# Attention fill work: halves ordered by the scalar engine's sequencer, transfers paced by exponentials, three vector-exponential stacks

## The chip, the cores and the metric

The kernel runs on one core of a Trainium2 chip. The core has TensorE (PE: matmuls), VectorE (DVE), ScalarE (ACT: exponentials), GpSimd (POOL, which here mostly issues transfers) and SyncE (SP, which issues the other transfers). Each engine works through its own list of instructions in order; between engines an instruction waits on semaphores. The metric is the device time of one execution, in microseconds (us).

## The reference

Two independent blocks share one output. Block A is attention with 32 query heads of width 16 over one common key and value head, for 2048 positions; block B is a short causal convolution, a product, and a long causal convolution done by Fourier transforms, for 512 channels.

```python
q = (x @ wq).reshape(B, S, H, Dh).transpose(0, 2, 1, 3)      # H = 32, Dh = 16, S = 2048
k = x @ wk; v = x @ wv                                       # one head for all
p = softmax(einsum("bhqd,bkd->bhqk", q, k) * Dh ** -0.5)
a = einsum("bhqk,bkd->bhqd", p, v).transpose(0, 2, 1, 3).reshape(B, S, H * Dh) @ wo
k_shift = sum(k_pad[:, t:t + S, :] * shift_k[:, 3 - t] for t in range(4))
kv = k_shift * v_B
y = irfft(rfft(kv, 2 * S) * rfft(ssm_k, 2 * S))[:S] + kv * ssm_D
out = concatenate([a, q_B * y], axis=-1)
```

## The kernel before

**Attention.** The 32 heads and 2048 queries are cut into 32 *stacks*. A stack is four heads by 512 queries, against 16 key tiles of 128 keys, so it has 32 *tiles* of 128 keys by 1024 query columns. For each tile PE makes the scores (eight matmuls, line 928) into one of two PSUM buffers `s`, ACT turns them into exponentials `p` (line 940, one instruction per tile), and some tiles later PE multiplies `p` with the values (line 964, "pv") into an accumulator pair `f`. After a stack's last tile VectorE copies the accumulator out (lines 973 and 974), and the sums and the unnormalised outputs go to DRAM. The loop `attend` writes this program one tile at a time; one pass of it is a *step*, and each step has one exponential. The two `s` buffers mean that the scores of tile t+1 wait until the exponential of tile t-1 is done.

**Fill work.** Everything else is written into the gaps of that loop by `_Fill`: the query projections, the transforms of block B (forward: `hT` and `a` against the table `ff`; backward: `sp` against `fi`), the output projection `wo`. Each of these is a Python generator, a "thread", that asks for PE matmul units or for VectorE time, or says `WAIT n`, which means 2n steps of nothing. `_Fill.turn` has a budget per step for PE and another for VectorE (850 ns per step). So the order on every engine is fixed when the program is written; nothing is rearranged at run time.

**Halves.** Most fill matmuls come through `halves` (line 243 is its matmul, line 255 its memset). A product is done as two halves: in the first, rows 0 to 63 of the PE array write one PSUM bank and rows 64 to 127 another; in the second half the two row groups change banks. The two row groups run side by side, so the second half may begin only when the last matmul of the first half is finished. The kernel orders this with a small VectorE memset of the tile `look`: the memset waits for the last matmul of the first half, and the first matmul of the second half waits for the memset. `yield WAIT, 0.5` puts the second half at least one step later.

**Vector exponentials.** In four stacks (`OWN_IN`, line 71) the last key tile's two exponentials are not made by ACT. The thread `own` (lines 1016 to 1027) has PE make those scores during the stack before, and VectorE evaluates a polynomial of degree five on them; `pv` then takes the result. Such a stack has 30 tiles for ACT instead of 32.

**Transfers.** POOL issues the loads of block B: the tables `ff` and `fi` (line 288), the long filter `hin` (line 316), rows of keys `kk` (lines 355 and 367), `tpb` (358), values `v` (380), gates `q` (442), and the stores `out` (463). SP issues the rest, among them the stack's queries `st` (884), the spill of two chunks of the transposed input to DRAM and its return (805, 811), and the small transfers of `heads`. A transfer is issued as soon as its queue reaches it and its buffer is free.

**Heads.** For each pair of stacks, `heads` loads the row sums `rl` and the outputs `of` from DRAM (1064, 1066), VectorE takes reciprocals (1070, 1071), these go to DRAM (`rd`, 1072) and come back spread over the partitions (`r`, 1077), and VectorE divides (1082). `WAIT` statements between these steps say how many steps later the consumer is written.

Of the kernel before, what the change touches and what calls it, by code (L numbers as in the profile page):

```python
# [8 lines left out]
F32 = mybir.dt.float32  # L9
# [4 lines left out]
AF = mybir.ActivationFunctionType  # L14
# [5 lines left out]
P = 128  # L20
# [3 lines left out]
DH = 16  # L24
NKT = S // P
NQ = 4 * H // 4
CB = 256
# [6 lines left out]
SC = XS * WS  # L34
# [28 lines left out]
LN2 = 0.6931471805599453  # L63
# [4 lines left out]

DOWN = 80
OWN = NKT - 1  # L70
OWN_IN = (27, 28, 29, 30)
OWN_AT, OWN_PV = 14, 8


# [31 lines left out]
WAIT = -1.0  # L106
# [3 lines left out]
class _Emit:  # L110
# [22 lines left out]
    def order(self, a, b):  # L133

        info = mybir.DependencyInfo(mybir.DependencyClass.Sync, mybir.DependencyReason.DATA)
        self.tc.add_manual_dep(a.ins, b.ins.name, info, reason="row halves change banks")

    def wide(self):
        return self.ps.tile([P, 2, 512], F32, tag="s", name=self.nm("x"))
# [87 lines left out]
    def halves(self, a, b, grain, dve=0):  # L227

        banks, look = [], None
        for half in range(2):  # L230
            n, k = 0, len(a)
            while n < k:
                g = yield (k - n) * grain, dve * half, CONT if banks else NEW, grain
                start = not banks
                if start:
                    f = self.pair()
                    banks += [f[:, 0, :], f[:, 1, :]]
                for m in range(n, n + g // grain):
                    for e in range(2):
                        out, (cols, w, x) = banks[half ^ e], (a, b)[half ^ e][m]  # L240
                        r = slice(64 * e, 64 * e + 64)
                        for j in range(0, P, 32):
                            y = self.nc.tensor.matmul(  # L243
                                out[j : j + 32, cols],
                                w[r, j : j + 32],
                                x[r],
                                start=half == m == 0,
                                stop=half == 1 and m == k - 1,
                            )
                            if look is not None:  # L250
                                self.order(y, look)
                                look = None
                n += g // grain
            if half == 0:
                look = self.nc.vector.memset(self.look, 0.0)  # L255
                self.order(look, y)
                yield WAIT, 0.5, CONT
        return banks
# [26 lines left out]
    def table(self, n, m2):  # L285
        t = self.w.tile([P, 2, 2, P], F32, tag="ft", bufs=FT, name=self.nm(n))
        for i in range(2):
            self.nc.gpsimd.dma_start(t[:, i], self.I[n][:, 2 * m2 + i])  # L288
        return t

    def s2(self, n, shape=(2, CB), dt=F32):
# [15 lines left out]
    def long_load(self, blk):  # L307

        nc = self.nc
        hin = self.w.tile([P, 8, 512], F32, tag="in", bufs=1, name=self.nm("hin"))  # L310
        for b in range(8):
            c0 = blk * CB + 32 * b
            for a in range(0, 4, 2):
                dst = hin[32 * a : 32 * a + 64, b, :]
                src = self.I["B_ssm_k"][c0 : c0 + 32, 512 * a : 512 * a + 1024].rearrange("r (a t) -> a r t", a=2)
                nc.gpsimd.dma_start(dst, src)
            yield WAIT, 1.5
        return hin

# [27 lines left out]
    def short_load(self, blk):  # L347
        nc, w = self.nc, self.w
        cs = slice(blk * CB, (blk + 1) * CB)
        tpb = w.tile([P, 4, CB], F32, tag="tp", bufs=1, name=self.nm("tpb"))  # L350
        kk = w.tile([P, 16, CB], F32, tag="in", bufs=1, name=self.nm("kk"))
        nc.gpsimd.memset(kk[0:1, 13:16, :], 0.0)
        for i in range(13, 16):
            for a, b in ((1, 16), (16, P)):
                nc.gpsimd.dma_start(kk[a:b, i, :], self.kr[a - 1 : b - 1, i, cs])
            yield WAIT, 0.5
        for i in range(4):
            nc.gpsimd.dma_start(tpb[:, i, :], self.skd[i : i + 1, cs].broadcast_to([P, CB]))
            yield WAIT, 0.5
        for m2 in range(2):  # L360
            self.rows(kk, blk, m2)
            yield WAIT, 0.5
        self.ld[blk] = tpb, kk

    def rows(self, kk, blk, m2):
        for i in (2 * m2, 2 * m2 + 1):
            self.nc.gpsimd.dma_start(kk[:, i, :], self.kr[:, i, blk * CB : (blk + 1) * CB])

    def short_products(self, blk, tpb, kk):

        nc, w = self.nc, self.w
        cs = slice(blk * CB, (blk + 1) * CB)
        for m2 in range(8):
# [19 lines left out]
            for i in (2, 1, 0):  # L393
                t = self.s2("t")
# [35 lines left out]
    def backward(self, blk, cx, places):  # L430

        nc, w = self.nc, self.w
        cs = slice(blk * CB, (blk + 1) * CB)
        g1, g2 = places
        ft, q = {i: self.table("fi", i) for i in range(2)}, {}

        def load(m2):
            if m2 > 1:
                ft[m2] = self.table("fi", m2)
            q[m2] = self.s2("q")  # L440
            for i in range(2):
                nc.gpsimd.dma_start(q[m2][:, i], self.qr[:, 2 * m2 + i, cs])

        load(0)
        load(1)
# [1 line left out]
        for m2 in range(8):  # L447
# [11 lines left out]
            b = yield from self.halves(*work, 2, 850)  # L459
# [265 lines left out]
    def prologue(self):  # L725
        nc = self.nc
# [6 lines left out]
        self.gm = self.c.tile([P, 18], F32, name="gm")  # L733
        nc.gpsimd.memset(self.gm, 0.0)
        self.qa, self.st, self.pt, self.qn, self.qs = {}, {}, {}, (0, 0), set()
        self.kst = self.c.tile([P, S], F16, name="kst")
        self.vx = self.c.tile([P, NKT, 32], F32, name="vx")
        self.look = self.c.tile([P, 4], F32, name="look")
# [61 lines left out]
    def spill(self):  # L800

        for c in range(2, 4):
            for i in range(8):
                yield WAIT, 0.5
                self.nc.sync.dma_start(self.xd[c - 2, :, i // 4, i % 4], self.xT[c][:, i // 4, i % 4])
        self.seen.add("spill")
        for c in range(2):
            yield from self.after(f"q{c}")
            for i in range(8):
                yield WAIT, 1  # L810
                self.nc.sync.dma_start(self.xT[c + 2][:, i // 4, i % 4], self.xd[c, :, i // 4, i % 4])
            self.seen.add(("x", c + 2))

    def hurry(self):
# [122 lines left out]
    def exp(self, u, s):  # L937

        self.pt[u] = self.w.tile([P, 2, 512], F32, tag="p", bufs=PB, name=self.nm("p"))
        self.nc.scalar.activation(self.pt[u], s, AF.Exp, scale=LN2 * DH**-0.5 / SC / SC)  # L940

    def pv(self, x, part, stop=False):

# [113 lines left out]
    def heads(self, G):  # L1057
# [18 lines left out]
        for i in range(0, 512, CB):  # L1076
            nc.sync.dma_start(r[:, i : i + CB], rows[:, i : i + CB].unsqueeze(1).broadcast_to([8, DH, CB]))
            yield WAIT, 1
        yield WAIT, 1.5
        for out, a, b, op in ((oc[:, 0], o, r, ALU.mult), (o, o, r, ALU.mult), (oc[:, 1], o, oc[:, 0], ALU.subtract)):  # L1080
            yield 0, 700
            nc.vector.tensor_tensor(out, a, b, op)
# [367 lines left out]
```

## Time and profile before

| what | value |
|---|---|
| time, median of 3 runs (lowest to highest) | 1049.73 us (1048.74 to 1056.47) |
| the profiled execution's own time | 1059.92 us |
| its span, first to last instruction | 1058.1 us |
| mean granted TensorE clock | 0.969 |
| PE / DVE / ACT / POOL busy | 960.1 / 760.1 / 955.2 / 171.3 us |
| exponentials (line 940) | 1016, 942.6 us busy, 66.1 us idle before them |

Busy time counts a stretch in which two instructions of an engine overlap once. The idle time of a group is what its engine stood still just before its instructions, with the releaser: the instruction whose semaphore ended most of it. An engine that is busy nine tenths of the time can still be waiting for another in the stretches that set the end, so the idle time in front of the exponentials, and what lies behind each piece of it, says more than the busy shares.

### The profile page before, as it was taken

How to read it: one execution, taken by the hardware profiler on the slowest of the kernel's cores; microseconds unless marked ns; L12 is line 12 of the kernel's file. 1: busy time of each engine (PE TensorE's matmuls, PEld its weight loads, DVE VectorE, ACT ScalarE, POOL GpSimd, SP SyncE). 2: the span in 40 equal slices, each digit the busy share in tenths (PEclk: the TensorE clock that was granted, in tenths of full speed). 3: DMA queues.
4: the chain of work that ended last, by engine and by line, in shares of the span. 5: the costliest groups of instructions: out<-in, count | busy, mean ns of one | idle time of the engine just before them, and what ended most of it. 6: DMA issues, size and time to landing. Idle time of an engine off the chain costs nothing.

```text
span 1058.1 us, 51250 instructions
## 1 busy us (share of the span) xinstructions
PE 960.1 (91%) x23455; PEld 469.8 (44%) x23455; DVE 760.1 (72%) x1094; ACT 955.2 (90%) x1032; POOL 171.3 (16%) x305
## 2 busy tenths in 40 slices
PE   8999998799998999899999989999889889888985
PEld 4345444344543444454444544444334344444452
DVE  4548854798536989888988657699898936775533
ACT  4799998699997999999998979999999998889883
POOL 2542214100031000012304243101000012201000
PEclk9899999899999999999999989999999999989998
DMA  6362435213142111212324243102211122210101
GB/s 227 117 188 75 140 90 116 67 52 96 48 108 64 61 45 51 65 57 71 116 72 140 83 129 101 51 29 64 84 40 32 60 71 66 87 59 28 46 4 43
DMA packets 69316, 83.11 MB, mean 79 GB/s; under 512 B 20800, under 2 KB 58278, under 8 KB 69094
## 3 DMA queue, kind: packets, MB, share of 16 engines
q1 hardware_dynamic: 47142, 43.51, 13.1%
q0 software_dynamic: 20320, 35.46, 11.9%
q8 instruction: 185, 3.03, 1.2%
q10 hardware_dynamic: 1632, 0.81, 0.3%
q14 instruction: 37, 0.30, 0.1%
HBM read 54.66 MB, written 25.03 MB: 75 GB/s over the span
## 4 chain that ended last, share of the span: by engine, by line
PE 36%; ACT 35%; issue 12%; DVE 11%; DMA 3%; POOL 2%; SPq 0%; ACTq 0%; POOLq 0%; DVEq 0%
ACT p L940 35%; PE f L964 16%; PE s L928 9%; PE f L243 8%; DVE sp L163 1%; DVE own L1027 1%; DVE ao L973 1%; DVE ao L974 1%; DVE sp L283 1%; DMA r<-rd 1%; DVE a L398 1%; POOL out L463 1%; DMA rd<-rl 1%; DMA xb<-in_A_x 1%; DVE t L389 1%
## 5 line engine op out<-in xcount | busy, mean ns | idle before, releaser
L940 ACT ACTIVATE p<-s 128x1024 f32<-128x1024 f32 x1016 | 942.6, 1064 | 66.1 <-PE s L928 62.9
L964 PE MATMUL f<-p,vx 64*32 64x512 f32 (+1 forms) x8880 | 561.3, 564 | 1.1 <-DVE sp L283 1.1
L928 PE MATMUL s<-st,kst 49*32 49x512 f16 x8128 | 432.1, 386 | 30.8 <-ACT p L940 26.1
L928 PEld LDWEIGHTS <-kst 49*32 49x32 f16 x8192 | 199.0, 91 | 392.3 <-issue 350.6
L964 PEld LDWEIGHTS f<-p,vx 64*32 64x32 f32 x8880 | 179.7, 108 | 37.6 <-issue 11.2
L163 DVE TENSOR_TENSOR sp<-sp 128x1024 f32<-128x1024 f32 x96 | 111.6, 1215 | 6.7 <-issue 6.1
L283 DVE COPY sp<-f 128x512 f32<-128x512 f32 x64 | 41.2, 685 | 42.4 <-PE f L243 42.0
L288 POOL DMA_DIRECT2D ff<-in_ff x64 | 34.3, 542 | 214.5 <-PE s L928 196.6
L463 POOL DMA_DIRECT2D out<-r x32 | 17.4, 550 | 287.0 <-DVE r L461 287.0
L243 PE MATMUL f<-wo,o 64*32 64x512 f16 x1440 | 56.6, 379 | 7.3 <-DVE look L255 6.0
L163 DVE TENSOR_TENSOR sp<-sp,sp 128x1024 f32<-128x1024 f32 x48 | 56.0, 1218 | 5.2 <-issue 3.9
L243 PE MATMUL f<-xT,wq 64*32 64x512 f16 x1344 | 51.8, 375 | 1.6 <-DVE look L255 1.2
L243 PE MATMUL f<-a,ff 64*32 64x256 f32 x1024 | 43.4, 386 | 9.2 <-DVE look L255 3.7
L243 PE MATMUL f<-hT,ff 64*32 64x256 f32 x1024 | 44.0, 381 | 8.5 <-issue 4.4
L243 PE MATMUL f<-sp,fi 64*32 64x256 f32 x1024 | 41.8, 387 | 9.8 <-DVE look L255 9.8
L973 DVE COPY ao<-f 128x512 f32<-128x512 f32 (+1 forms) x33 | 22.2, 673 | 29.5 <-PE f L964 29.4
L398 DVE TENSOR_TENSOR a<-a,t 128x512 f32<-128x512 f32 x48 | 33.1, 690 | 11.9 <-issue 10.2
L461 DVE TENSOR_TENSOR r<-f,q 128x256 f32<-128x256 f32 x32 | 12.1, 419 | 33.7 <-PE f L243 33.6
L389 DVE TENSOR_TENSOR t<-kk,tpb 128x512 f32<-128x512 f32 (+1 forms) x50 | 33.0, 662 | 3.0 <-issue 2.7
L380 POOL DMA_DIRECT2D v<-in_B_v x32 | 17.0, 537 | 100.3 <-DVE a L400 36.1
L243 PEld LDWEIGHTS <-o 64*32 64x32 f16 x1440 | 21.7, 93 | 23.2 <-DVE look L255 7.4
L243 PEld LDWEIGHTS f<-hT,ff 64*32 64x32 f32 x1024 | 20.9, 107 | 21.4 <-issue 9.1
(166 smaller groups left out, 751.0 us busy)
## 6 DMA issues: line engine op xcount, KB each, us to landing
ff<-in_ff POOLq DMA_DIRECT2D x64, 128.0 KB, 3.7
od<-ao SPq DMA_DIRECT2D x60, 128.0 KB
qd<-qp SPq DMA_DIRECT2D x48, 128.0 KB
st<-qd SPq DMA_DIRECT2D x62, 98.0 KB
kk<-in_B_k POOLq DMA_DIRECT2D x32, 128.0 KB, 3.8
v<-in_B_v POOLq DMA_DIRECT2D x32, 128.0 KB, 3.2
hin<-in_B_ssm_k POOLq DMA_DIRECT2D x32, 128.0 KB, 7.5
fi<-in_fi POOLq DMA_DIRECT2D x32, 128.0 KB, 3.0
```

What stands on the lines that cost most here:

```text
L163: v.tensor_tensor(part(out), part(a), part(b), op)
L243: y = self.nc.tensor.matmul(out[j : j + 32, cols], w[r, j : j + 32], x[r], start=half == m == 0, stop=half == 1 and m == k - 1,)
L283: self.nc.vector.tensor_copy(c[:, :, m + i, :], b[i].rearrange("p (q n) -> p q n", q=2))
L288: self.nc.gpsimd.dma_start(t[:, i], self.I[n][:, 2 * m2 + i])
L380: nc.gpsimd.dma_start(v[:, i], self.vr[:, 2 * m2 + i, cs])
L389: nc.vector.tensor_tensor(out[:, n], kk[:, x], tap(i, n.stop - n.start), ALU.mult)
L398: nc.vector.tensor_tensor(a, a, t, ALU.add)
L463: nc.gpsimd.dma_start(self.orr[:, 2 * m2 + i, D + blk * CB : D + (blk + 1) * CB], r[:, i])
L928: self.nc.tensor.matmul(s[j : j + 32, e, :], self.kst[rows, k * P + j : k * P + j + 32], self.st[n][rows, a, cols], start=True, stop=True,)
L940: self.nc.scalar.activation(self.pt[u], s, AF.Exp, scale=LN2 * DH**-0.5 / SC / SC)
L964: nc.tensor.matmul(self.acc[e][32 * j : 32 * j + 32, m], vx[rows, :], y, start=k == 0, stop=stop)
L973: nc.vector.tensor_copy(a, self.acc[0][:, m])
```

## The change

Four edits, made together:

1. In `halves` the memset on VectorE becomes `nc.scalar.nop()`, written at the same place. In the program it is a semaphore instruction of ACT's own sequencer: it waits for the last matmul of the first half and then raises a semaphore of the sequencer, for which the second half's first matmul waits. There are 69 of them. The tile `look` goes.
2. A helper `paced` adds a wait to the loads of block B and to the spill: the transfer waits for the exponential written two before the newest one at the place where the transfer is written. It is applied to `ff`, `fi`, `hin`, `kk`, `tpb`, `v`, `q` on POOL and to the spill and its return on SP. Stores and the stack's queries are not paced.
3. `OWN_IN` loses stack 27, so that stack's two last tiles are exponentials of ACT: 1018 in place of 1016.
4. In `heads`, for the first eight pairs (G up to 7), the wait before the reciprocals grows from 4 to 10 steps and the wait before the divisions from 3 to 12 steps. For later pairs both are as before.

```diff
-OWN_IN = (27, 28, 29, 30)
+OWN_IN = (28, 29, 30)
...
+    def paced(self, dma):
+
+        u = max(self.pt, default=0)
+        if u > 2:
+            self.order(dma, self.exps[(u - 2) % 4])
...
             if half == 0:
-                look = self.nc.vector.memset(self.look, 0.0)
+                look = self.nc.scalar.nop()
                 self.order(look, y)
                 yield WAIT, 0.5, CONT
...
-            self.nc.gpsimd.dma_start(t[:, i], self.I[n][:, 2 * m2 + i])
+            self.paced(self.nc.gpsimd.dma_start(t[:, i], self.I[n][:, 2 * m2 + i]))
...
-                nc.gpsimd.dma_start(dst, src)
+                self.paced(nc.gpsimd.dma_start(dst, src))
...
-                nc.gpsimd.dma_start(v[:, i], self.vr[:, 2 * m2 + i, cs])
+                self.paced(nc.gpsimd.dma_start(v[:, i], self.vr[:, 2 * m2 + i, cs]))
...
-                self.nc.sync.dma_start(self.xd[c - 2, :, i // 4, i % 4], self.xT[c][:, i // 4, i % 4])
+                self.paced(self.nc.sync.dma_start(self.xd[c - 2, :, i // 4, i % 4], self.xT[c][:, i // 4, i % 4]))
...
-        self.nc.scalar.activation(self.pt[u], s, AF.Exp, scale=LN2 * DH**-0.5 / SC / SC)
+        self.exps[u % 4] = self.nc.scalar.activation(self.pt[u], s, AF.Exp, scale=LN2 * DH**-0.5 / SC / SC)
...
-        yield WAIT, 2
+        yield WAIT, 5 - 3 * (G > 7)
...
-        yield WAIT, 1.5
+        yield WAIT, 6 - 4.5 * (G > 7)
```

The first place is VectorE's list during the preparation of the vector exponentials of stack 28 (`own` are their operands, `r` the gated outputs of the backward transform, `ao` a finished stack's output). Before:

```order
L1024 TENSOR_SCALAR x_20079<-own_15239 128x1024
L1027 SCALAR_TENSOR_TENSOR own_15239<-own_15240 128x1024
L973 COPY ao_20131<-f_19603 128x512
L974 TENSOR_TENSOR ao_20131<-ao_20131,f_19603 128x512
L1027 SCALAR_TENSOR_TENSOR own_15239<-own_15239,own_15240 128x1024 x2
L255 MEMSET look 128x4
L1027 SCALAR_TENSOR_TENSOR own_15239<-own_15239,own_15240 128x1024
L1027 SCALAR_TENSOR_TENSOR own_15239<-own_15239,x_20079 128x1024
L1024 TENSOR_SCALAR x_20241<-own_15239 128x1024
L1027 SCALAR_TENSOR_TENSOR own_15239<-own_15240 128x1024
```

And now, at the same work:

```order
L1030 TENSOR_SCALAR x_19936<-own_16574 128x1024
L1033 SCALAR_TENSOR_TENSOR own_16574<-own_16575 128x1024
L1033 SCALAR_TENSOR_TENSOR own_16574<-own_16574,own_16575 128x1024 x3
L1033 SCALAR_TENSOR_TENSOR own_16574<-own_16574,x_19936 128x1024
L1030 TENSOR_SCALAR x_20081<-own_16574 128x1024
L467 TENSOR_TENSOR r_19823<-f_20000,q_19443 128x256 x2
L979 COPY ao_20159<-f_19590 128x512
L980 TENSOR_TENSOR ao_20159<-ao_20159,f_19590 128x512
L1033 SCALAR_TENSOR_TENSOR own_16574<-own_16575 128x1024
```

The memset no longer stands between the polynomial's instructions; the copies out of PSUM moved a few places, and the polynomial is unbroken.

The second place is PE's list where the backward transform (`sp` against `fi`) begins its second half, behind the scores of a tile (`kst`). Before:

```order
L928 LDWEIGHTS kst
L928 MATMUL s_20178<-st_19612,kst 32x512
L243 MATMUL f_20148<-sp_13571,fi_19499 32x256 [waits DVE_49]
L243 MATMUL f_20148<-sp_13571,fi_19499 32x256 x7
L928 LDWEIGHTS kst
L928 MATMUL s_20197<-st_19612,kst 32x512 [waits Activation_49]
```

And now:

```order
L934 LDWEIGHTS kst
L934 MATMUL s_20206<-st_19599,kst 32x512
L249 MATMUL f_20176<-sp_13670,fi_19561 32x256 [waits Activation_sequencer_49]
L249 MATMUL f_20176<-sp_13670,fi_19561 32x256 x7
L934 LDWEIGHTS kst
L934 MATMUL s_20226<-st_19599,kst 32x512 [waits Activation_49]
```

Only the semaphore changed: VectorE's before, that of ACT's sequencer now. The next tile's scores stand behind the second half in both.

The third place is POOL's list where the first half of the long filter is loaded (`hin`). Before:

```order
L316 DMA hin_3818<-in_B_ssm_k 64x1x512 [waits DMASW2_49,DVE_49]
L316 DMA hin_3818<-in_B_ssm_k 64x1x512 [waits DMASW3_49]
L316 DMA hin_3818<-in_B_ssm_k 64x1x512 [waits DMASW4_49]
L316 DMA hin_3818<-in_B_ssm_k 64x1x512 [waits DMASW5_49]
L316 DMA hin_3818<-in_B_ssm_k 64x1x512 [waits DMASW6_49]
```

And now:

```order
L322 DMA hin_3844<-in_B_ssm_k 64x1x512 [waits DMASW2_49,DVE_49,Activation_49]
L322 DMA hin_3844<-in_B_ssm_k 64x1x512 [waits DMASW3_49]
L322 DMA hin_3844<-in_B_ssm_k 64x1x512 [waits DMASW4_49,Activation_49]
L322 DMA hin_3844<-in_B_ssm_k 64x1x512 [waits DMASW5_49]
L322 DMA hin_3844<-in_B_ssm_k 64x1x512 [waits DMASW6_49,Activation_49]
```

Nothing moved; each pair of loads now also waits for an exponential, and successive pairs for exponentials three apart.

More of the change, by code (lines that the diff above doesn't have):

```diff
@@ L354, in short_load @@
             for a, b in ((1, 16), (16, P)):
-                nc.gpsimd.dma_start(kk[a:b, i, :], self.kr[a - 1 : b - 1, i, cs])
+                self.paced(nc.gpsimd.dma_start(kk[a:b, i, :], self.kr[a - 1 : b - 1, i, cs]))
             yield WAIT, 0.5
         for i in range(4):
-            nc.gpsimd.dma_start(tpb[:, i, :], self.skd[i : i + 1, cs].broadcast_to([P, CB]))
+            self.paced(nc.gpsimd.dma_start(tpb[:, i, :], self.skd[i : i + 1, cs].broadcast_to([P, CB])))
             yield WAIT, 0.5
@@ L366, in rows @@
         for i in (2 * m2, 2 * m2 + 1):
-            self.nc.gpsimd.dma_start(kk[:, i, :], self.kr[:, i, blk * CB : (blk + 1) * CB])
+            self.paced(self.nc.gpsimd.dma_start(kk[:, i, :], self.kr[:, i, blk * CB : (blk + 1) * CB]))
     def short_products(self, blk, tpb, kk):
@@ L441, in load @@
             for i in range(2):
-                nc.gpsimd.dma_start(q[m2][:, i], self.qr[:, 2 * m2 + i, cs])
+                self.paced(nc.gpsimd.dma_start(q[m2][:, i], self.qr[:, 2 * m2 + i, cs]))
         load(0)
@@ L735, in prologue @@
         self.qa, self.st, self.pt, self.qn, self.qs = {}, {}, {}, (0, 0), set()
+        self.exps = [None] * 4
         self.kst = self.c.tile([P, S], F16, name="kst")
         self.vx = self.c.tile([P, NKT, 32], F32, name="vx")
-        self.look = self.c.tile([P, 4], F32, name="look")
         nc.gpsimd.memset(self.vx, 1.0)
@@ L810, in spill @@
                 yield WAIT, 1
-                self.nc.sync.dma_start(self.xT[c + 2][:, i // 4, i % 4], self.xd[c, :, i // 4, i % 4])
+                self.paced(self.nc.sync.dma_start(self.xT[c + 2][:, i // 4, i % 4], self.xd[c, :, i // 4, i % 4]))
             self.seen.add(("x", c + 2))
```

## The prediction

> **What bounds the kernel now.** I read the page first, then the line of the exponentials by itself, then the list of waits. The page gives busy time and, behind the second bar, idle time and who ended it:
>
> ```profile
> span 1058.1 us, 51250 instructions
> ...
> PE 960.1 (91%) x23455; PEld 469.8 (44%) x23455; DVE 760.1 (72%) x1094; ACT 955.2 (90%) x1032; POOL 171.3 (16%) x305
> ...
> L940 ACT ACTIVATE p<-s 128x1024 f32<-128x1024 f32 x1016 | 942.6, 1064 | 66.1 <-PE s L928 62.9
> ```
>
> ```profile
> L940 ACT ACTIVATE p<-s x1016: 1007/1077/1112, 31.1 to 1038.8; 128x1024 f32<-128x1024 f32 x170
> L940 ACTq EVENT_SEMAPHORE  x950: 17/17/17, 35.3 to 1038.7; - x190
> ```
>
> The exponentials run from 31.1 to 1038.8 us, and one starts 0.92 us after the other where nothing holds them (a row below has nine in 8.41 us: less one of 1.06, eight distances of 0.92). They are the chain that must be got through: 1016 x 0.92 = 935 us out of 1009. The remaining 74 us are the 66.1 us of idle time, nearly all of it ended by PE's scores, and what a broken chain loses at each restart: a lone one takes 1.02 to 1.06, so about 0.14 more. The 31 us ahead and the 18 behind are not touched by the change. So the question is what makes PE late with scores:
>
> ```profile
> ACT p L940 <- PE s L928: 62.9, 45, 9.4
> ...
> DVE look L255 <- PE f L243: 34.9, 13, 6.4
> ...
> PE s L928 <- ACT p L940: 26.1, 73, 0.5
> PE f L243 <- DVE look L255: 23.5, 15, 3.1
> ...
> DVE o L1082 <- DMA r<-rd: 13.3, 3, 10.9
> ```
>
> PE waits 23.5 us for the memset `look`, though a memset takes 0.06 us. One of the fifteen places, with all engines, shows why:
>
> ```profile
> 875.27 8.41 ACT L940 ACTIVATE p<-s 128x1024 f32<-128x1024 f32 x9
> ...
> 881.32 0.67 PE L243 MATMUL f<-sp,fi 64*32 64x256 f32 x16
> ...
> 881.91 0.41 PE L928 MATMUL s<-st,kst 49*32 49x512 f16 x8
> ...
> 883.13 1.23 DVE L1027 SCALAR_TENSOR_TENSOR own<-own,own 128x1024 f32<-128x1024 f32 x1
> 884.30 0.06 DVE L255 MEMSET look<- 128x4 f32 x1
> 884.39 2.49 DVE L1027 SCALAR_TENSOR_TENSOR own<-own,own 128x1024 f32<-128x1024 f32 x2
> 884.44 1.11 PE L243 MATMUL f<-sp,fi 64*32 64x256 f32 x16 [2.12 <-DVE look L255]
> ...
> 886.07 1.02 ACT L940 ACTIVATE p<-s 128x1024 f32<-128x1024 f32 x1 [2.39 <-PE s L928]
> ```
>
> The first half is over at 881.99, but VectorE is still in the polynomial, in order, and reaches the memset at 884.30. PE stands 2.12 us, the scores behind it come late, and ACT stands 2.39.
>
> **Term 1: the halves, -26 us.** The nop takes the memset's place, in ACT's list directly behind the newest exponential. It cannot hold ACT: the matmul it waits for stands ahead of the scores for which the next exponential waits anyway. Its price is that of the 950 semaphore rows above, 17 ns, and such a row already stands ahead of nearly every exponential without stretching the 0.92 us: 69 x 17 ns = 1.2 us, hidden behind the running exponential. If it broke the overlap instead it would cost 69 x 0.14 = 10 us; I take 0. Nor should PE wait for it: the second half stands behind a later tile's scores, most often two tiles later, and those scores need an exponential older than or equal to the one ahead of the nop.
>
> So the stops should go. On ACT's side they are twenty idle times at fourteen places. The first two and the last:
>
> ```profile
> 161.21 1.94 ACT L940 ACTIVATE p<-s 128x1024 f32<-128x1024 f32 x2 [2.38 <-PE s L928]
> 163.77 1.03 ACT L940 ACTIVATE p<-s 128x1024 f32<-128x1024 f32 x1 [0.62 <-PE s L928]
> ...
> 1009.96 3.02 ACT L940 ACTIVATE p<-s 128x1024 f32<-128x1024 f32 x3 [0.52 <-PE s L928]
> ```
>
> They sum to 28.0 us; with twenty restarts of 0.14 that is 30.8, the upper end. But VectorE is as busy as before, and at those places up to 3 us behind. It must still copy the finished pair out of PSUM, and PE, no longer held at mid-pair, may wait for that copy at the next pair. Between a second half and the next first half lie at least two steps, 1.8 us, so only lags above that come back; the longest wait for `look` is 3.1. I give back about 1.2 us at each of the four stops of 2 to 3 us in the last 180 us: 4.8. Term: **-26**; lower end -14, if half came back.
>
> **Term 2: a transfer that holds VectorE, -10.4 us.**
>
> ```profile
> 178.88 9.17 DMA r<-rd
> ...
> 188.17 0.70 DVE o L1082
> ```
>
> ```profile
> 191.57 0.61 PE L701 MATMUL f<-qa,wb 128*32 128x512 bf16 x1 [9.49 <-DVE sp L283]
> ...
> 192.87 1.02 ACT L940 ACTIVATE p<-s 128x1024 f32<-128x1024 f32 x1 [9.36 <-PE s L928]
> ```
>
> The load of `r` took 9.17 us. VectorE stood at the division for it (the 10.9 in the list of waits), the PSUM copies of `sp` stood behind the division, and PE stood behind those. The change writes the division nine steps later for these pairs, 8.3 us, which leaves 2.6 of the 10.9; PE only began to stand at 182.1, 4.8 us after VectorE, so nothing remains. ACT's 9.36 and the 0.99 after it go: **-10.4**. Lower end -5, if the load is slower still.
>
> **Term 3: loads in a burst, -3 us.**
>
> ```profile
> 305.42 5.94 POOL L316 DMA_DIRECT2D hin<-in_B_ssm_k  x9 [12.43 <-DVE hT L337]
> ...
> 318.44 0.65 POOL L316 DMA_DIRECT2D hin<-in_B_ssm_k  x1 [0.36 <-DMA hin<-in_B_ssm_k]
> ```
>
> ```profile
> 315.12 0.66 PE L243 MATMUL f<-hT,ff 64*32 64x256 f32 x14
> 320.17 0.37 PE L243 MATMUL f<-hT,ff 64*32 64x256 f32 x1 [4.38 <-issue]
> ```
>
> ```profile
> 321.14 1.02 ACT L940 ACTIVATE p<-s 128x1024 f32<-128x1024 f32 x1 [4.56 <-PE s L928]
> 323.55 3.03 ACT L940 ACTIVATE p<-s 128x1024 f32<-128x1024 f32 x3 [1.39 <-PE s L928]
> ```
>
> PE stops after 14 of 16 matmuls of one group, where it has nothing to wait for ("issue"), amid sixteen loads of 128 KB in 13.7 us. That looks like PE's own instructions arriving late behind the burst. Paced, the loads come two per three exponentials, so sixteen take 7 x 2.75 = 19 us or more: three tenths thinner, and longer. ACT's cost was 4.56 + 1.39 = 5.95. I count half, **-3**; ends -6 (gone) and +6 (it happens again). The Trainium skill, "Runtime: NRT & Kernel Launch", section "Instruction fetch mechanics", says that an engine streams its instructions in 16 KiB blocks by DMA, at a cost that is mostly hidden. By that rule the stop has another cause, the term is 0 and the sum 3 us less; the idle 4.38 us in mid-group speaks against "hidden" here.
>
> **Term 4: what is added, +2.8 us.** Two exponentials: 2 x 0.92 = +1.8. PE does the same matmuls. VectorE loses the polynomial:
>
> ```profile
> 0.00:1059.00 1059.00, 5.37 (x128) 2.75 (x128) 73.39 (x64) 0.97 0.27 78
> ```
>
> This counts only what touches `own`: 73.39 us for four stacks, 18.3 for one. It was on the path only as the lag behind `look`, so it is counted in term 1. Pacing can make a load late:
>
> ```profile
> ff<-in_ff POOLq DMA_DIRECT2D x64, 128.0 KB, 3.7
> ...
> v<-in_B_v POOLq DMA_DIRECT2D x32, 128.0 KB, 3.2
> ```
>
> ```profile
> L288 POOL DMA_DIRECT2D ff<-in_ff x64: 536/536/600, 56.1 to 657.8; - x64
> ```
>
> A table needs 2 x 0.54 to issue and 3.7 to land, 4.8 us. The program writes it at least ten steps (9.2 us) ahead of its matmul, but for the first table of the second short transform, two steps ahead, which is late already:
>
> ```profile
> 611.58 1.08 POOL L463 DMA_DIRECT2D out<-r  x2 [5.98 <-DVE r L461]
> ...
> 612.65 2.13 POOL L288 DMA_DIRECT2D ff<-in_ff  x4
> ...
> 615.47 1.35 PE L243 MATMUL f<-a,ff 64*32 64x256 f32 x16 [3.33 <-DMA ff<-in_ff]
> ```
>
> That stop stays. The values `v` are closest: five or six steps (4.6 to 5.5 us) against two `kk` and two `v` issues and 3.2, together 5.3. VectorE may stand up to 0.7 us in each of 16 rounds: 0 to +11; it no longer stands 34.9 us at `look`, which covers most, so I take +1. Behind a paced transfer on POOL stand the `out` stores, for which nobody waits soon; on SP stand `st` loads, written 26 steps ahead, mostly.
>
> **Sum.** -26 - 10.4 - 3 + 2.8 = -36.6, against the profiled execution's own 1059.9: 1023. That execution is 10.2 us above the median, and the three runs differ by 7.7 among themselves. If the excess is general, the median goes to 1013. If it lies in the transfers of terms 2 and 3, which the change mostly removes, it goes to 1023. Nothing in one trace tells which. I take **1015**, nearer the first, since the three runs' lower two agree within 1 us.
>
> **The rivals.**
>
> *VectorE's lag only moves.* All of term 1 comes back as waits for copies out of PSUM (`sp`, `r`, `cut`). For it: VectorE does the same work in the same order, and is 97% busy (its third sum, 38.95 of 40 us) in this stretch:
>
> ```profile
> 760.00:800.00 40.00, 33.82 (x848) 15.47 (x840) 38.95 (x42) 38.41 (x43) 0.00 (x0) 1.00 0.17 54
> ```
>
>  Against it: the list of waits has VectorE standing 34.9 us at `look` for PE, time it now has. Time: 1015 + 26 = **1041**, chance 0.12.
>
> *Contention stays.* The stretched loads still delay `r` and PE's instructions, so terms 2 and 3 give nothing: 1015 + 13 = **1028**, chance 0.13. The rule on instruction fetch gives a quarter of this.
>
> *The nop is slow.* ACT's sequencer passes it only when the exponential ahead is done, and overlap breaks: +10, and PE waits up to 0.5 us (0.92 less the scores' 0.41) where the second half follows one tile later, about one in six of 69: +6. Time **1031**, chance 0.07. The rows of 17 ns that fall inside a running exponential speak against it.
>
> *Paced tables come late (the slower side).* Pacing ties each of 48 table pairs (64 + 32 loads) to PE's own progress, so a lag cannot be made up. Each one as late as that at 612 costs 3.3 us. From eleven on (36.6 / 3.3) the gain is gone; with sixteen late the time is 1015 + 53 = **1068**. It decides once issue and landing take over 9.2 us, against 4.8 in the rows. Chance 0.08.
>
> **How the numbers follow.** The forecast itself has 0.60, its own range 1000 to 1030. About 1% (10 us) is what a measurement can tell from no change, so faster means below 1039. Forecast, contention and slow nop are faster, and the moved lag sits on the border, half and half: faster 0.86, same 0.06, slower 0.08. The range may leave out no more than 0.2. Its low end is 1000: term 1 at 30.8, term 3 at 6 and `v` free take 9 off, a general excess of the profile 2, and 4 are for lags of `sp` copies that shrink with VectorE's freed time. Its high end is 1041, where the moved lag lies; only late tables and the tails stay outside.
>
> **What would show it.** In the changed profile: no line waits for VectorE at the second half's matmul; ACT's idle time falls from 66 to about 30; the semaphore rows at the nop take 17 ns; no stop of over 5 us near 183; VectorE's count falls by 85. Wrong would be: PE idle ended by `sp`, `r` or `cut` copies by more than 10 us in total, `DMA ff` or `fi` as the releaser of many matmuls, or exponentials more than 0.92 us apart where a nop stands.

## The result, and the profile after

The changed kernel took **1015.07 us** (median of four runs, 1014.1 to 1016.7) against 1049.24 for the kernel before beside it (four runs, 1043.55 to 1056.47): a ratio of 0.967, 95% interval [0.961, 0.973]. The forecast was 1015, range 1000 to 1041. The profiled execution of the changed kernel took 1014.1 us, its span is 1012.3.

The page of the changed kernel, the rows that answer those shown of before: span, busy time, and the exponentials (now line 946) with their idle time behind the second bar.

```profile
span 1012.3 us, 51279 instructions
...
PE 947.4 (94%) x23439; PEld 463.1 (46%) x23439; DVE 738.7 (73%) x1009; ACT 953.3 (94%) x1034; POOL 172.0 (17%) x305
...
L946 ACT ACTIVATE p<-s 128x1024 f32<-128x1024 f32 x1018 | 940.8, 1068 | 22.2 <-PE s L934 19.3
```

ACT's idle time before the exponentials fell from 66.1 to 22.2 us, 43.9 of the 45.8 us between the two profiled executions. The 1018 exponentials are as busy as the 1016 were. VectorE issues 85 instructions fewer (1094 to 1009). The mean granted TensorE clock is 0.989, against 0.969 before.

From the list of waits of the changed kernel (who waits for whom: total us, times, longest). No row has PE waiting for a look back (the order between two halves, by the memset of `look` before); the longest rows that bear on the exponentials are these.

```profile
PE s L934 <- ACT p L946: 27.6, 72, 0.5
ACT p L946 <- PE s L934: 19.3, 22, 3.4
PE f L249 <- DMA ff<-in_ff: 3.4, 1, 3.4
```

The line of the nop by itself (count, duration least/median/most, and who waited for it):

```profile
L261 ACTq EVENT_SEMAPHORE  x69: 17/17/17, 69.1 to 988.3; - x69
...
  PEld f L249: 1.2, 6
```

All 69 take 17 ns, and PE's weight loads wait for them six times, 1.2 us in all. In the trace each starts 0.05 to 0.12 us after the matmul that it waits for has ended; of the 69 memsets in the first profile of before, 23 came more than 0.2 us after it, the latest 3.4. Where no idle time lies between, exponentials with one of these nops between them start 0.92 us apart at the mean, like the others. The Trainium skill, "PSUM — Partial Sum Buffer", section "Engine vs sequencer instructions", says that a sequencer passes a nop once the instructions ahead are dispatched, not when they are complete; by that rule the nop does not wait out the exponential ahead of it, and the trace agrees: 68 of the 69 ran before that exponential had ended, at the median 0.66 us before.

Two stretches of the timeline of the changed kernel (start, length, engine, line, work, count; in brackets the idle time ahead and what ended it). The first covers both the stop at 161 and the place of the long stop at the division; the second lies in the polynomial of a vector-exponential stack, the kind of place where the memset used to come late.

```profile
149.46 37.24 ACT L946 ACTIVATE p<-s 128x1024 f32<-128x1024 f32 x40
```

```profile
867.65 14.84 ACT L946 ACTIVATE p<-s 128x1024 f32<-128x1024 f32 x16
868.17 1.22 DVE L1033 SCALAR_TENSOR_TENSOR own<-own 128x1024 f32<-128x1024 f32 x1
868.24 0.63 PE L249 MATMUL f<-sp,fi 64*32 64x256 f32 x16
869.43 3.74 DVE L1033 SCALAR_TENSOR_TENSOR own<-own,own 128x1024 f32<-128x1024 f32 x3
870.08 0.63 PE L249 MATMUL f<-sp,fi 64*32 64x256 f32 x16
```

Forty exponentials in 37.24 us and sixteen in 14.84 are 0.93 us each, with no idle time between them. What remains of ACT's idle time is the start, one stop at 590 us, one of 2.44 and 1.05 us near 975, and short ones where PE waited for VectorE to take a result out of PSUM. The first and the last of these short ones:

```profile
344.43 0.63 PE L249 MATMUL f<-xT,wq 64*32 64x512 f16 x16 [0.96 <-DVE gm L729]
345.41 2.10 ACT L946 ACTIVATE p<-s 128x1024 f32<-128x1024 f32 x2 [0.73 <-PE s L934]
...
914.30 0.62 PE L249 MATMUL f<-wo,o 64*32 64x512 f16 x16 [1.62 <-DVE r L467]
915.27 1.03 ACT L946 ACTIVATE p<-s 128x1024 f32<-128x1024 f32 x1 [1.39 <-PE s L934]
```

There are five (0.73, 1.15, 0.62, 0.74, 1.39): 4.6 us. A sixth, 0.82 us at 951, stands behind the polynomial (`own`). The stop at 590 is the late first table of the second short transform:

```profile
588.91 2.13 POOL L294 DMA_DIRECT2D ff<-in_ff  x4
...
591.83 0.68 PE L249 MATMUL f<-a,ff 64*32 64x256 f32 x12 [3.42 <-DMA ff<-in_ff]
...
593.04 1.02 ACT L946 ACTIVATE p<-s 128x1024 f32<-128x1024 f32 x1 [3.43 <-PE s L934]
```

### The profile page after: what moved, and what is told of

It reads as the page before. It is cut to its first block, busy times and chain, and to the rows that moved or that the text cites. A ratio compares the mean times of both kernels' runs of the same rounds, so it can differ in the third digit from the quotient of the medians.

```text
span 1012.3 us, 51279 instructions
## 1 busy us (share of the span) xinstructions
PE 947.4 (94%) x23439; PEld 463.1 (46%) x23439; DVE 738.7 (73%) x1009; ACT 953.3 (94%) x1034; POOL 172.0 (17%) x305
## 4 chain that ended last, share of the span: by engine, by line
PE 56%; ACT 27%; DVE 9%; issue 7%; DMA 2%; POOL 0%; SPq 0%; ACTq 0%; DVEq 0%; POOLq 0%
ACT p L946 26%; PE f L970 26%; PE s L934 16%; PE f L249 12%; DVE own L1033 2%; DVE sp L169 1%; DMA xb<-in_A_x 1%; DVE ao L979 1%; PE x L231 0%; PE f L617 0%; DVE u L218 0%; DVE sp L289 0%; DVE sp L219 0%; DVE sp L220 0%; DVE ao L980 0%
## 5 line engine op out<-in xcount | busy, mean ns | idle before, releaser
L946 ACT ACTIVATE p<-s 128x1024 f32<-128x1024 f32 x1018 | 940.8, 1068 | 22.2 <-PE s L934 19.3
L970 PE MATMUL f<-p,vx 64*32 64x512 f32 (+1 forms) x8896 | 554.0, 556 | 1.7 <-DVE cut L683 1.1
L979 DVE COPY ao<-f 128x512 f32<-128x512 f32 (+1 forms) x33 | 22.2, 673 | 50.3 <-PE f L970 50.3
L294 POOL DMA_DIRECT2D fi<-in_fi x32 | 17.6, 555 | 187.1 <-ACT p L946 187.1
L249 PE MATMUL f<-a,ff 64*32 64x256 f32 x1024 | 43.4, 382 | 4.6 <-DMA ff<-in_ff 3.4
L467 DVE TENSOR_TENSOR r<-f,q 128x256 f32<-128x256 f32 x32 | 12.1, 419 | 45.2 <-PE f L249 45.2
L249 PE MATMUL f<-hT,ff 64*32 64x256 f32 x1024 | 41.5, 377 | 1.2 <-PE s L934 0.3
L322 POOL DMA_DIRECT2D hin<-in_B_ssm_k x32 | 21.1, 665 | 58.8 <-ACT p L946 57.4
```

What stands on the lines that cost most here:

```text
L249: y = self.nc.tensor.matmul(out[j : j + 32, cols], w[r, j : j + 32], x[r], start=half == m == 0, stop=half == 1 and m == k - 1,)
L294: self.paced(self.nc.gpsimd.dma_start(t[:, i], self.I[n][:, 2 * m2 + i]))
L322: self.paced(nc.gpsimd.dma_start(dst, src))
L946: self.exps[u % 4] = self.nc.scalar.activation(self.pt[u], s, AF.Exp, scale=LN2 * DH**-0.5 / SC / SC)
L970: nc.tensor.matmul(self.acc[e][32 * j : 32 * j + 32, m], vx[rows, :], y, start=k == 0, stop=stop)
L979: nc.vector.tensor_copy(a, self.acc[0][:, m])
```

## The experiments

Kernels of one group ran on one chip beside the same runs of the kernel before. All of them compute the whole reference. "Idle" is ACT's idle time before the exponentials in the profile of that run; it was 66.1 in the first profile of before and 22.2 after.

| kernel | time, us | ratio to before | idle, us |
|---|---|---|---|
| *group 1 (before 1052.4)* | | | |
| changed kernel | 1016.12 | 0.9649 [0.9613, 0.9684] | 24.5 |
| memset put back | 1035.62 | 0.9847 [0.9809, 0.9884] | 35.6 |
| pacing taken out | 1022.88 | 0.9698 [0.9650, 0.9747] | 28.8 |
| short waits in `heads` | 1019.09 | 0.9686 [0.9650, 0.9723] | 26.1 |
| *group 2 (before 1052.79)* | | | |
| nop alone | 1034.38 | 0.9829 [0.9772, 0.9886] | 43.4 |
| pacing alone | 1038.57 | 0.9874 [0.9830, 0.9918] | 42.5 |
| three stacks alone | 1048.14 | 0.9947 [0.9922, 0.9971] | 53.1 |
| three stacks and long waits | 1039.89 | 0.9885 [0.9835, 0.9936] | 41.1 |
| *group 3 (before 1054.47)* | | | |
| changed kernel | 1017.71 | 0.9646 [0.9614, 0.9678] | 25.0 |
| 556 more nops | 1029.98 | 0.9762 [0.9732, 0.9793] | 29.0 |
| earlier first tables | 1010.08 | 0.9572 [0.9547, 0.9597] | 17.4 |
| kernel before, second profile | 1050.64 (one run) | | 56.2 |

### The changed kernel again

> The changed kernel once more, as the reference for the others of this group: 1015 us, ratio 0.967 to the kernel before. No theory is tested by it.

It gave 1016.12 us; this is the base of the three that follow.

### The memset put back

```diff
-                look = self.nc.scalar.nop()
+                look = self.nc.vector.memset(self.look, 0.0)
```

> The changed kernel with the vector memset of the tile look back in place of the nop, all else as changed. Theory (halves): the stops behind look come back, less the one in stack 27, whose polynomial is gone: 1015 + 23 = 1038 us, ACT idle before exponentials 22 -> 45 us or more, PE waits for look about 20 us. Rival (contention: the gain came from pacing and the moved divisions): within 5 us of 1015.

Measured: 1035.62, **+19.5 us**; the intervals do not touch. The waits show where (the memset is line 261 here):

```profile
ACT p L947 <- PE s L935: 32.3, 31, 4.2
PE f L249 <- DVE look L261: 15.7, 11, 2.8
```

PE waits for the memset 15.7 us, not the 23.5 of before; three stacks alone, below, bring it down as well. ACT's idle time grows by 11.1 (24.5 to 35.6) and its busy time by 2.6 (940.7 to 943.3), together a little more than the 12.1 us between the two spans (1016.8 to 1028.9). The profiled execution was the quickest of its five, that of the changed kernel the slowest of its four; the other 7 us between the medians are in executions without a profile.

### Pacing taken out

```diff
-        if u > 2:
+        if u > 1 << 30:
```

> The changed kernel without pacing: every transfer is issued as soon as its queue and buffer allow. Theory (halves): 1015 + 3 = 1018 us, at most 1025; a mid-group stop of PE of some 4 us beside the burst of hin loads may be back. Rival (contention): 1015 + 13 = 1028 us or more, with the load of r slow again.

Measured: 1022.88, +6.8 us, but the intervals overlap (0.9650 to 0.9747 against 0.9613 to 0.9684). No long stop came back at the division, only this:

```profile
182.01 1.98 ACT L946 ACTIVATE p<-s 128x1024 f32<-128x1024 f32 x2
185.07 5.61 ACT L946 ACTIVATE p<-s 128x1024 f32<-128x1024 f32 x6 [1.08 <-PE s L934]
```

There are two more: one of 1.64 us at 310, which the changed kernel's profiles do not have, and one of 2.16 at 375 for a VectorE copy (`cut`), where they have 1.15. So with the divisions written late, pacing is worth a few microseconds at most, not the ten of the long stop.

### Short waits in heads

```diff
-        yield WAIT, 5 - 3 * (G > 7)
+        yield WAIT, 2
...
-        yield WAIT, 6 - 4.5 * (G > 7)
+        yield WAIT, 1.5
```

> The changed kernel with the short waits of heads back for all pairs. Theory: the stop of 9.4 us at the division comes back only if the load of r is slow again; paced loads leave it shorter, so 1015 + 5 = 1020 us, between 1015 and 1025. Rival (the moved division alone was worth 10 us): 1025 us, with VectorE standing 10 us for r near 180 us.

Measured: 1019.09, +3.0 us, not to be told from nothing. The waits of this run, and its timeline over the place of the long stop:

```profile
DVE o L1088 <- DMA r<-rd: 8.9, 5, 2.4
```

```profile
149.23 51.83 ACT L946 ACTIVATE p<-s 128x1024 f32<-128x1024 f32 x56
```

VectorE again stands at divisions, 2.4 us at most, but ACT runs 56 exponentials without a break. With paced loads the short waits alone do not make the stop that term 2 was about.

### The nop alone

```diff
-                look = self.nc.vector.memset(self.look, 0.0)
+                look = self.nc.scalar.nop()
```

> The kernel before with the nop in place of the memset and nothing else. Theory (halves): 1049 - 26 = 1023 us, ratio 0.975; PE's waits for look are gone, ACT idle 66 -> about 38 us. Rival (VectorE's lag only moves): within 5 us of 1049, with PE waiting for copies of sp, r and cut instead.

Measured: 1034.38, **-18.4 us**. The look back is gone from the waits, but the stop at the division is longer. Its wait, the issue of the load, and ACT:

```profile
DVE o L1082 <- DMA r<-rd: 27.5, 4, 16.2
```

```profile
L1077 SPq DMA_DIRECT2D r<-rd x2: 572/582/592, 175.4 to 176.1; - x2
```

```profile
194.41 1.02 ACT L940 ACTIVATE p<-s 128x1024 f32<-128x1024 f32 x1 [12.19 <-PE s L928]
```

The load was issued some 3 us earlier than before (175.4 against 178.25), and the division still began later (189.7 against 188.17). ACT stood 12.19 us there instead of 9.36. That loss hides some 3 us of what the nop gains. Four stops of 1.46 to 1.69 us (477, 906, 937 and 968 us), which the changed kernel does not have, look like VectorE's lag come back: two of them end with a VectorE instruction (`sp`, `wp`), for the other two the profile names nothing.

### Pacing alone

```diff
+    def paced(self, dma):
...
-            self.nc.gpsimd.dma_start(t[:, i], self.I[n][:, 2 * m2 + i])
+            self.paced(self.nc.gpsimd.dma_start(t[:, i], self.I[n][:, 2 * m2 + i]))
...
```

> The kernel before with pacing and nothing else. Theory (halves): the mid-group stop at 316 us and part of the stop at 183 us go: 1049 - 6 = 1043 us, ratio 0.994 (0.985 to 1.00). Rival (contention): 1049 - 16 = 1033 us, ratio 0.985 or less. Rival (paced tables late): above 1049 us, PE waiting for ff and fi.

Measured: 1038.57, **-14.2 us**. The look back stays as it was, and both stops that I had put down to transfers are gone, the one at the division although the division is written as early as before:

```profile
PE f L249 <- DVE look L261: 23.4, 15, 3.1
...
DVE o L1089 <- DMA r<-rd: 4.3, 3, 2.2
```

```profile
160.81 1.94 ACT L947 ACTIVATE p<-s 128x1024 f32<-128x1024 f32 x2 [2.30 <-PE s L935]
163.37 37.40 ACT L947 ACTIVATE p<-s 128x1024 f32<-128x1024 f32 x40 [0.62 <-PE s L935]
```

Why `r` comes sooner shows in what POOL's queue (software_dynamic) took of the 16 DMA engines between 165 and 192 us, of before and of pacing alone (packets, MB, share):

```profile
q0 software_dynamic: 4735, 3.18, 56.9%
```

```profile
q0 software_dynamic: 2188, 1.13, 15.6%
```

Sixteen loads of the long filter and eight of a table were issued in that stretch before; with pacing it is ten of the filter, and the queue takes 15.6% in place of 56.9%. The load of `r` was not all that was held up: from the issue of the small write `rd` to that of `r`, which needs it, it is 7.3 us before and 1.4 with pacing.

### Three stacks alone, and with long waits in heads

```diff
-OWN_IN = (27, 28, 29, 30)
+OWN_IN = (28, 29, 30)
```

The second run takes the long waits of `heads` as well, as in the change.

> The kernel before with vector exponentials in stacks 28 to 30 and nothing else. Theory: two more exponentials +1.8 us, and the stop of 3.2 us behind look in stack 27 gone: 1049 - 1 = 1048 us, ratio 0.998 to 1.002. Rival (the polynomial was on the path for more than that stop): ratio 0.99.

> The kernel before with the longer waits of heads and vector exponentials in stacks 28 to 30. Theory: the stop of 10.4 us at the division goes, and the own part gives -1: 1049 - 11 = 1038 us, ratio 0.989, and no stop over 5 us near 183 us. Rival (what held the division is only met later): within 3 us of 1048.

The first gave 1048.14, -4.7 us, with the longest waits for the memset gone:

```profile
PE f L243 <- DVE look L255: 12.7, 11, 2.0
```

That is 10.8 us less than the 23.5 before, although this edit adds two exponentials. The stop at the division stayed (9.26 us). The second gave 1039.89, -12.9 us, so the long waits are worth 8.2 beside the three stacks; in its profile the stop at the division is gone and the one in mid-group is still there:

```profile
306.73 0.65 PE L249 MATMUL f<-hT,ff 64*32 64x256 f32 x13
311.13 0.64 PE L249 MATMUL f<-hT,ff 64*32 64x256 f32 x2 [3.75 <-issue]
...
312.72 1.02 ACT L947 ACTIVATE p<-s 128x1024 f32<-128x1024 f32 x1 [4.73 <-PE s L935]
```

The long waits with four stacks were not run, so what they give by themselves is not measured.

### Many more nops

```diff
...
+                if self.relay is not None:
+                    self.order(self.newest, self.relay)
+                    self.relay = None
...
+            if pvs:
+                self.relay = self.nc.scalar.nop()
+                self.order(self.relay, self.newest)
```

> The changed kernel with 556 more of the nops on ACT: one behind the exponential of every step that has value matmuls, waiting for the newest of these, and the next step's first value matmul waits for it. Nothing needs that order, so only the price of the relay is seen. My theory (17 ns each, passed while an exponential runs): time within 3 us of the changed kernel, about 1016, ratio to the kernel before 0.965, exponentials still 0.92 us apart. Rival (a nop breaks the overlap of two exponentials, 0.14 us each, or PE waits for it): 556 x 0.14 = 78 us more, about 1094, ratio 1.04.

Measured: 1029.98 against 1017.71 beside it, **+12.3 us**, 22 ns for each of the 556. Neither number on record holds: the rival's 78 us are far off, and so is "within 3". The profile has the exponentials and the line of the added nop, with who waited for it:

```profile
L947 ACT ACTIVATE p<-s 128x1024 f32<-128x1024 f32 x1018 | 948.1, 1056 | 29.0 <-PE s L935 23.5 <-ACT p L947 0.6 <-PE f L249 0.4
```

```profile
L1064 ACTq EVENT_SEMAPHORE  x556: 17/17/17, 43.4 to 1008.9; - x186
...
  PEld f L971: 71.6, 152
```

Each still takes 17 ns, but PE's weight loads waited for 152 of them, 71.6 us in all and up to 1.1 each. The nop itself is not late: each of the 556 starts 0.04 to 0.13 us after the matmul that it waits for has ended. But the matmul that waits for it follows only one step behind, so PE's weight load now stands until the value matmuls of the step before are finished. ACT pays as well: it stands 4.0 us more, and its busy time is 7.1 us longer (948.1 against 941.0); exponentials with an added nop between them start 0.94 us apart at the mean, the others 0.92. The 69 nops of the change stand mostly two tiles ahead of their waiter. At 22 ns each they would cost 1.5 us.

### The kernel before, profiled again

> The kernel before, unchanged, profiled a second time, to see which of its stops vary. If the first profile's 10 us above the median lie in the two stops ascribed to transfers (ACT's 9.4 us near 183 and 4.6 + 1.4 near 316), this profile has a shorter span, about 1048, and these stops are shorter while the stops at the look back (PE 23.5 us) stay within 3 us. If the excess is general, the stops are the same and the distance of the exponentials or the granted clock differs.

One run, 1050.64 us, with a span of 1048.7, which is 9.4 less than in the first profile. Its exponentials, and ACT at the two stops:

```profile
L940 ACT ACTIVATE p<-s 128x1024 f32<-128x1024 f32 x1016 | 942.3, 1063 | 56.2 <-PE s L928 52.5 <-ACT p L940 1.0
```

```profile
192.06 1.02 ACT L940 ACTIVATE p<-s 128x1024 f32<-128x1024 f32 x1 [7.26 <-PE s L928]
194.19 2.98 ACT L940 ACTIVATE p<-s 128x1024 f32<-128x1024 f32 x3 [1.11 <-PE s L928]
...
321.67 2.98 ACT L940 ACTIVATE p<-s 128x1024 f32<-128x1024 f32 x3 [0.88 <-PE s L928]
```

The stop at the division is 8.4 us in place of 10.35, the one near 320 is 0.88 in place of 5.95: 7.1 of the 9.4 us. The look back is the same (22.7 us against 23.5). So the first profile was slow chiefly in the two stops ascribed to transfers. The granted clock differs as well (0.969 and 0.977), which was on record as a sign of a general excess; but in the first profile it is 0.60 from 182 to 193 us, over the stop at the division, and 1.00 from 200 to 206, so its mean goes with the stops. What the lower clock adds to a restart was not separated.

### Earlier first tables

```diff
-        ft = {i: self.table("ff", i) for i in range(2)}
+        ft = self.early if blk else {i: self.table("ff", i) for i in range(2)}
...
+            if m2 == 6 and blk == 0:
+                self.early = {i: self.table("ff", i) for i in range(2)}
```

> The changed kernel with the first two ff tables of the second short transform loaded two rounds earlier, while the backward transform of the first half still runs. Theory (the stop near 589 is a late load and nothing else): ACT's 3.43 + 0.79 + 0.38 us there go, 1016 - 4.6 = 1011.5, ratio to the kernel before 0.960. Rival (the earlier tables push the backward transform's own tables back on POOL's queue, or PE finds no other work there): no gain, 1016, ratio 0.965, with a stop of the same length within 20 us of the old place.

> The changed kernel again, as the reference beside the other three: 1016, ratio to the kernel before 0.965, span about 1014.

Measured: 1010.08 against 1017.71 for the changed kernel beside it; the intervals of the ratios do not touch. The gain of 7.6 us is more than the 4.6 on record. In the timeline with the earlier tables (the loads are those of `ff`), and in that of the changed kernel of the same group, ACT at this place:

```profile
559.16 61.00 ACT L948 ACTIVATE p<-s 128x1024 f32<-128x1024 f32 x66
...
575.14 1.08 POOL L294 DMA_DIRECT2D ff<-in_ff  x2
```

```profile
595.49 1.03 ACT L946 ACTIVATE p<-s 128x1024 f32<-128x1024 f32 x1 [3.91 <-PE s L934]
597.62 1.02 ACT L946 ACTIVATE p<-s 128x1024 f32<-128x1024 f32 x1 [1.10 <-PE s L934]
598.90 1.02 ACT L946 ACTIVATE p<-s 128x1024 f32<-128x1024 f32 x1 [0.26 <-PE s L934]
```

The stop is gone. In the profile beside it, it was 5.3 us rather than 4.6. Between these two profiles ACT's idle time fell by 7.6 us (25.0 to 17.4); of the other 2.3, 1.3 lie in the stop near 978 us (3.6 against 2.35 with the earlier tables, the cause is open), the rest in short ones. Each of these two kernels ran six times. This version beats both kernels: 0.957 of before.

## Why the prediction was right, and where it was not

**The bound.** It held: the time followed ACT's idle time (43.9 of 45.8 us between the profiles).

**Term 1, -26.** It covered the nop and, as said in term 4, the lag from the fourth stack's polynomial. The memset put back costs 19.5; three stacks alone gain 4.7, which is 6.5 once the two exponentials at 1.8 are taken off. Together 26.0. The agreement is closer than the runs can support (they come from different groups, and the nop alone gave 18.4), but the size is right. So is the size of the give-back: 4.8 was put, and the five short stops behind VectorE make 4.6 (5.4 with the one behind `own`). That is partly luck, for they are not at the four places I named; only one of the five lies in the last 180 us. What was wrong inside the term is the share of the edits: the stack taken out halved the waits for the memset by itself, so it does part of what I gave to the nop.

**Term 2, -10.4.** The amount is right and the reason too narrow. I wrote that the division nine steps later removes the stop. It does (three stacks and long waits: no stop). But pacing alone removes it as well, since it takes the loads away that slowed `r`, and `rd` before it, which the term left out (7.3 us to 1.4). Each of two edits would have sufficed, which is one reason why the parts do not add: -18.4 for the nop, -14.2 for pacing and -12.9 for the other two make -45.5, and all together give -36.3 in group 1. Between the two sums lie 9.2 us. The stop at the division (8.4 to 10.4 us in the two profiles of before) is in two of the parts, the lag of the fourth polynomial (6.5) in two as well, and the nop alone lost some 3 us at the division; that would make 12 to 14, so the parts are known to a few microseconds only.

**Term 3, -3.** In each of the six profiles with unpaced loads ACT stands behind one of its 285th to 291st exponentials (308 to 326 us), from 0.88 to 4.73 us; in the eight with paced loads it stands there 0.69 us at most. That pacing removes the stop is well supported. Its price in an ordinary execution is not the 5.95 of the first profile: half of the six are under 2.3, so the half that the term counted was not far off.

That PE's instructions come late, which the term only supposed, the traces bear out. Two rows: the queue of instruction blocks over the whole first profile of before, and PE in the second profile.

```profile
q8 instruction: 185, 3.03, 1.2%
```

```profile
321.18 0.39 PE L928 MATMUL s<-st,kst 49*32 49x512 f16 x2 [0.69 <-issue]
```

The queue moved 185 blocks of 16 KB, one for every 254 of PE's 46,910 matmuls and weight loads, which are nine tenths of the program, so it is PE's list that it brings. In all six profiles PE stands at this stage with nothing to wait for, 0.69 to 4.38 us: in three after 13 or 14 of 16 matmuls of a fill group (the first profile of before, pacing taken out, and three stacks with long waits), in three after six of the eight score matmuls of a tile. What stands there differs, but its place in PE's list does not: 13506 of PE's records (matmuls, weight loads, semaphore rows) lie ahead of the stop in five, and 257 fewer, about one block, in the first profile of before.

In each of the six PE goes on 1.4 to 2.5 us after a block of q8 has landed. At the median a block lands 1.8 us after PE has passed the seam one block earlier. Ahead of these six stops that took 5.0 to 7.9 us, and with paced loads 3.6 at most at the three seams of this stage. So PE stands at the seam of two blocks because the next one is late beside the loads. The longest wait shows in the queues of the first profile of before, where no block began between 307.5 and 316.5 us (the stop began at 315.8); in the second profile, with as dense a burst from 307 to 316.5, one did:

```profile
q0 software_dynamic: 2548, 1.33, 67.8%
```

```profile
q0 software_dynamic: 2505, 1.37, 73.3%
q8 instruction: 1, 0.02, 0.6%
```

The rule weighed in term 3 (the Trainium skill, "Runtime: NRT & Kernel Launch", section "Instruction fetch mechanics": the cost of the fetch is mostly hidden) fits most of the 185 blocks and not these six stops, so the measurement decides for the term. Why the block landed 7.7 us after its seam in one execution of the kernel before and 5.0 in the other stays open.

**Term 4, +2.8.** Two exponentials more did not lengthen ACT's busy time (942.6 to 940.8), which fits fewer broken chains and so more overlap (with three stacks alone, where most stops stayed, it grew by 1.7 to 944.3). The late `v` loads make VectorE wait 2.5 us in two places, with no stop of ACT there. The stop for `ff` stayed, as written.

**The last step, from the sum to the time.** Here two errors cancel. Against its own base, the profiled execution, the sum was 9 us too small: 45.8 and not 36.6 came off. Term 3 is 3.0 of that; four idle times of 0.61 to 0.75 us between 249 and 340 in the first profile of before, which I had not counted, are 2.7 more and are gone too; the `v` loads are 1.0. Of the remaining 2.5, ACT's busy time has 0.8 (it fell by 1.8, where 2.8 for restarts less 1.8 for two exponentials were to make 1.0); the rest lies in short idle times that I did not follow. And the excess of that execution was not general, as I assumed when I chose 1015 over 1023; 7.1 of 9.4 us lay in the stops of terms 2 and 3. By my own rule that would have been 1023. Against an ordinary execution the gain is 34 to 37 us, as the sum had it, since there the transfer stops are shorter. That the forecast met 1015 so closely is luck.

**The rivals.** *VectorE's lag only moves*: the waits that came instead are 5.4 us, not 26. *Contention stays*: refuted by pacing alone, where both stops went. *The nop is slow*: refuted for the 69, but its second half (PE waits where the user follows a tile later) is real, as the 556 show, and there it is the matmul ahead of the nop that makes PE wait, not the exponential. *Paced tables late*: one stop for `ff`, where it was before.

## What to carry to other kernels

In this kernel an ordering between two engines' instructions cost what was queued ahead of the relay, up to 3.4 us, not the 17 or 62 ns that the relay itself takes: choose an engine whose list is not behind at that place, and put the waiter two tiles back. When two edits both cure the same stop, parts measured alone add up to more than the whole, so look in each profile for the stop itself. Before pricing a stop that hangs on transfers, profile the kernel a second time: here one such stop was 5.95 us in one execution and 0.88 in the next.

## What the runs showed of the hardware that I had not expected

- A load of 128 KB issued by SP (`r`), and a write of 16 KB ahead of it (`rd`), slow with the traffic of POOL's queue: from the issue of `rd` to that of `r` it was 7.3 us beside the burst and 1.4 with the loads paced, and VectorE waited up to 16.2 us for `r` beside the burst and 2.4 at most without it, at the same size.
- A semaphore instruction of 17 ns on ACT's sequencer, placed behind 556 exponentials, cost 22 ns each, part of it as 7.1 us less overlap between exponentials, although it always ran within 0.13 us of the matmul that it waited for.
- PE stood up to 4.38 us in the middle of a group of matmuls with nothing to wait for, at the seam of two 16 KB blocks of its instructions: a block landed 1.8 us after the seam before it at the median, and 5.0 to 7.9 us after it amid a burst of loads.
